# Penalties on another engine, low parts straight from the transposes, weight halves in pieces: one change to a fused FFT, gated-MLP and expert kernel

## The chip, the core and the metric

The kernel runs on one core of a Trainium2 chip. A core has five engines that run their own instruction streams and wait for each other by semaphores: PE (matmul; its weight loads are listed apart as PEld), DVE (vector), ACT (scalar, activation), POOL (GpSimd) and SP, which here only issues DMAs. The metric is the device time of one execution in microseconds; each kernel is run several times and the median counts. Lower is better.

## The reference

Three layers in a row, all in fp32. `B, S, D = 8, 3072, 256`, so 24,576 tokens of width 256.

```python
X = np.fft.fft(np.fft.fft(x, axis=1), axis=2).real          # (8, 3072, 256)
x = X.reshape(24576, 256)
g = x @ w_gate; y = (g * sigmoid(g) * (x @ w_val)) @ w_out   # hidden width 1536
logits = y @ gate2                                           # 8 experts
# experts fill up greedily: all (token, expert) pairs in falling order of logit,
# a token goes to the first expert that has room, each expert takes 24576/8 = 3072
for e in range(8):
    out[mask_e] = np.maximum(y[mask_e] @ w1[e], 0) @ w2[e]   # 256 -> 1024 -> 256
```

## The kernel before, in words

**Numbers as two parts.** Matmul operands are split into a rounded high part and a remainder, the low part (`hi = cast(x)`, `lo = x - hi`), and each product is the sum of three matmuls: high by high, high by low, low by high. So nearly every operand needs a cast (on ACT) and a subtraction (on POOL or DVE) before PE can read it.

**Phase 1** (48 tiles of 512 rows; 0 to about 1957 us) does the transforms, the gated MLP and the logits. A tile has 12 steps, one for each 128 hidden units. In a step PE computes the products `Q` and `Pp` and, three steps late, the output product of an earlier step into four PSUM tiles `Y`; DVE combines (`T`, `G`, `hh`), ACT does the Silu and the cast `hi`, POOL the subtraction `lo` (L691). After the twelfth step `finish(t, u)` runs for u = 0 to 3: ACT copies `Y` to `ys`; POOL copies the 8 logits into `Lall` (L425) and writes the token's number into column 256 of the row (L427); SP stores 128 rows to the DRAM table `yscr` (L430). POOL also does the folds of the next batch's input (`fa`, `fb`, `z`) and the low part `xl` of the next tile.

**Phase 2.** A search on DVE with small matmuls finds the threshold of the first expert to close, and the list of its 3072 tokens. From then on the eight experts run one after the other on PE, and the search for the next experts runs beside them. An expert has six groups of 512 tokens. For a group, POOL gathers 4 times 128 rows of `yscr` by index (L1075); `transpose` (L1081) turns them on PE into PSUM, ACT copies them to SBUF (`yt`) and casts (`yh`), POOL subtracts (`yl`, L1099); eight `up` products (L1111) with Relu on ACT (`hh`, L1117) and a low part on DVE (`hl`, L1128) follow, then four `down` products (L1137), whose results ACT copies and POOL scatters to the output (L1146). The weights of the next expert come by two gathers of 1 MB (`load_w`, L1059) and are split in eight pieces of 512 columns (`split_w`: cast on ACT, L1068; subtraction on POOL, L1069).

**The order of the work** is written out in program order, each engine in order. The search and the listing are generators; `go(time)`, called twice in an `up` and four times in a `down`, adds to a credit (at most 1.3) and runs a step of each generator while the credit lasts; a step yields its cost. An expert can't begin until its listing is done: at the end of the sixth group a loop calls `go(1.0)` until it is (the forced rest, `while ph + 1 not in ready`), ahead of that group's `down`s. When an expert is chosen, `close` (L1006) adds the penalty of the experts that are closed to all 24,576 x 8 logits, one POOL instruction (L1009), for the next search to read. The listing has 12 items: PE looks a row up (L1036), DVE turns it into two indices (`j`, `le`, `idx`, L1039 to L1047).

Of the kernel before, what the change touches and what calls it, by code (L numbers as in the profile page):

```python
# [9 lines left out]
F32 = mybir.dt.float32  # L10
F32R = mybir.dt.float32r
BF16 = mybir.dt.bfloat16
I32 = mybir.dt.int32
# [74 lines left out]
def phase1(ctx, tc, io, yscr, Lall, ident, idt, NT, choice=None):  # L88
# [321 lines left out]
    def out_proj(g):  # L410
# [4 lines left out]
        for u in range(4):  # L415
            for i, (a, d) in enumerate(((0, 0), (0, 1), (1, 0))):
                nc.tensor.matmul(Yp[t][u], h[a][:, u * P : (u + 1) * P], Wo[c // 2][:, c % 2, d, :], start=(c == 0 and i == 0), stop=(c == NF - 1 and i == 2))  # L417

    def finish(t, u):
        hf, q = (t // 3) % 2, t % 3  # L420
        pp = Yp[t][u]
        ys = work.tile([P, EXT], F32, tag="ys", bufs=4, name="ys")
        nc.scalar.copy(ys, pp)
        c = 4 * t + u
        nc.gpsimd.tensor_copy(Lall[:, c, :], ys[:, D:EXT])  # L425

        nc.gpsimd.tensor_copy(ys[:, D : D + 1].bitcast(I32), idt[:, c : c + 1])  # L427

        n = P - 1 if hf == 0 and q == 0 and u == 2 else P
        nc.sync.dma_start(yscr[c * P : c * P + n, :], ys[0:n, :])  # L430


    def mini_tile():

        xs = {}
        r0 = work.tile([1, B], F32, tag="tz", bufs=1, name="t15r")
        nc.sync.dma_start(r0, t15scr.rearrange("b o -> o b"))
        for n in ("R", "T"):
            for a in range(2):
                xs[n, a] = work.tile([P, P], F32R, tag=f"m{n}{a}", bufs=1, name=f"m{n}{a}")  # L440
                nc.gpsimd.memset(xs[n, a].bitcast(F32), 0.0)
        hs = [[work.tile([P, 4, P], F32R, tag=f"z{2 * j + a}", bufs=2, name=f"hT{a}") for a in range(2)] for j in range(3)]
        for t in hs:
            for a in range(2):
                nc.gpsimd.memset(t[a].bitcast(F32), 0.0)
        yield
        yield
        for n, src, k in (("R", mini["R"], P), ("T", r0, 1)):
            nc.vector.tensor_copy(xs[n, 0][0:k, 0:B], src)
            nc.vector.tensor_sub(xs[n, 1][0:k, 0:B], src, xs[n, 0][0:k, 0:B].bitcast(F32))  # L450
        yield
        for j in range(3):
            sl = work.tile([P, 4, D], F32, tag="xs", bufs=2, name="xs").rearrange("p a b -> p (a b)")
            for gv in range(2):
                pp = bank("F", 1)
                n = 0
                for cs, k in ((0, "R"), (1, "T")):
                    for a, d in order:
                        nc.tensor.matmul(pp, xs[k, d], Wb[j][:, cs, gv, a, :], start=(n == 0), stop=(n == 5))
                        n += 1  # L460
                yield
                if gv == 0:
# [12 lines left out]
        for _ in range(4):
            yield
        pp = bank("F", 1)
        for c in range(NF):
            for i, (a, d) in enumerate(((0, 0), (0, 1), (1, 0))):
                nc.tensor.matmul(pp[:, 0:EXT], hs[c // 4][a][:, c % 4, :], Wo[c // 2][:, c % 2, d, :], start=(c == 0 and i == 0), stop=(c == NF - 1 and i == 2))  # L480
            if c % 4 == 3 and c < NF - 1:
                yield
                yield
        yield
        ys = work.tile([B, EXT], F32, tag="ys", bufs=4, name="ysm")
        nc.vector.tensor_copy(ys, pp[0:B, 0:EXT])
        lm = work.tile([B, E], F32, tag="lm", bufs=1, name="lm")
        nc.vector.tensor_copy(lm, ys[:, D:EXT])
        nc.vector.tensor_copy(ys[:, D : D + 1].bitcast(I32), idt[0:B, NCOL : NCOL + 1])
        nc.sync.dma_start(yscr[3 * P - 1 : N : S, :], ys)  # L490
        nc.sync.dma_start(Lall[P - 1 : P, 2 : 4 * NT : 24, :], lm)
# [308 lines left out]
def phase2(ctx, tc, io, yscr, Lall, ident, first, out):  # L800
# [47 lines left out]
    def search(ph, res):  # L848
# [117 lines left out]
        if ph < E - 1:  # L966
            shut = rp.tile([P, E], F32, tag="shut", name="shut")
            nc.vector.tensor_scalar(shut, code8, best, -3.3e38, ALU.is_equal, ALU.mult)
            nc.vector.tensor_add(pen, pen, shut)
            if ph > 0:  # L970
                close(res)
        yield 1.2

        ise = rp.tile([P, NCOL], F32, tag="ise", name="ise")
# [31 lines left out]
    def close(res):  # L1006

        ml = rp.tile([P, NCOL, E], F32, tag="ml", name="ml")
        nc.gpsimd.tensor_add(ml, Lall, across(pen, NCOL))  # L1009
        res["next"] = ml  # L1010

    def listing(ph, res, first=None):
# [17 lines left out]
            yield 0.3  # L1030
        res["idx"] = []
        for i in range(NS // 2):
            pl = bank("A", 3) if first else bank("L", 1)
            v = pl.rearrange("p (a c) -> p a c", a=2)
            for a in range(2):
                nc.tensor.matmul(v[:, a, 0:XW], on[:, 2 * i + a, :], x, start=True, stop=True)  # L1036
            yield 0
            j = rp.tile([P, 2], F32, tag="j", bufs=2, name="j")
            nc.vector.tensor_sub(j, siota[:, 2 * i : 2 * i + 2], v[:, :, NCOL])  # L1039
            cc = rp.tile([P, 2], F32, tag="cc", bufs=2, name="cc")  # L1040
            for a in range(2):
                le = rp.tile([P, NCOL], F32, tag="le", bufs=2, name="le")
                nc.vector.tensor_scalar(le, v[:, a, 0:NCOL], j[:, a : a + 1], None, ALU.is_le, ALU.add, accum_out=cc[:, a : a + 1])
            if i % 2 == 0:
                res["idx"].append(rp.tile([P, 4], I32, tag=f"idx{i // 2}", bufs=2, name=f"idx{i // 2}"))
            k = 2 * (i % 2)
            nc.vector.scalar_tensor_tensor(res["idx"][-1][:, k : k + 2], cc, float(P), v[:, :, NCOL + 1], ALU.mult, ALU.add)  # L1047
            if first and i % 2:
                first(i // 2)
            yield 1.5  # L1050


    scat = []
    spacer = const.tile([P, 1], F32, name="spacer")

# [7 lines left out]
    def split_w(res, n):  # L1063

        j = len(res[f"w{n}"])
        f = res[f"w{n}f"][:, j * 512 : j * 512 + 512]
        h = wp.tile([P, 2, 512], F32R, tag=f"w{n}", bufs=5, name=f"w{n}")
        nc.scalar.copy(h[:, 0, :], f)  # L1068
        nc.gpsimd.tensor_sub(h[:, 1, :], f, h[:, 0, :].bitcast(F32))  # L1069
        res[f"w{n}"].append(h)  # L1070

    def gather(res, i):
# [5 lines left out]
            )  # L1078
        res["yg", i] = yg

    def transpose(res, i, k, first=False):  # L1081
        if k == 0:
            res["y", i] = tuple(work.tile([P, 2, 512], F32R, tag=t, bufs=2, name=t) for t in ("yh", "yl"))
        hi, lo = res["y", i]
        yg = res["yg", i]
        pt = bank("A", 3)
        for s in range(4):
            nc.tensor.transpose(pt[:, s * P : (s + 1) * P], yg[:, s, k * P : (k + 1) * P], ident)  # L1088
        if k == 1:
            res["id", i] = work.tile([P, 4], I32, tag="id", bufs=3, name="id")  # L1090
            nc.scalar.copy(res["id", i], yg[:, :, D].bitcast(I32))
        if first:
            nc.scalar.copy(hi[:, k, :], pt)
            nc.vector.tensor_sub(lo[:, k, :], pt, hi[:, k, :].bitcast(F32))
            return
        yt = work.tile([P, 512], F32, tag="yt", bufs=2, name="yt")
        nc.scalar.copy(yt, pt)
        nc.scalar.copy(hi[:, k, :], yt)
        nc.gpsimd.tensor_sub(lo[:, k, :], yt, hi[:, k, :].bitcast(F32))  # L1099

    order = ((0, 0), (1, 0), (0, 1))

# [77 lines left out]
    def begin(i):  # L1180
        if i == 0:
            gather(exp[0], 0)
            close(exp[0])

    for _ in listing(0, exp[0], begin):
        pass
    for _ in range(4):
        split_w(exp[0], 2)
    for k in range(2):
        transpose(exp[0], 0, k, True)  # L1190
    sides = [lists(), searches()]

    credit = 0.0

    def go(time):
# [7 lines left out]
    for ph in range(E):  # L1203
# [3 lines left out]
        for i in range(6):  # L1207
            if i < 5:
                gather(cur, i + 1)
            for f in range(8):  # L1210
# [8 lines left out]
                    since = 8 * i + f  # L1219

                if loaded:
                    for n, lag, free in ((1, 4, 1 if i < 5 else min(4, 1 + (f + 1) // 2)), (2, 8, 1)):
                        if 8 * i + f > since + lag and len(nxt[f"w{n}"]) < free:
                            split_w(nxt, n)
                if i == 5 and ph + 1 in ready and ("yg", 0) not in nxt:
                    gather(nxt, 0)
            if i == 5 and nxt is not None:
# [73 lines left out]
```

## Time and profile before

| | us |
|---|---|
| median of 3 runs | 3296.31 (3295.22 to 3297.11) |
| the profiled execution | 3293.48 |
| its span, first to last instruction | 3291.7 |
| phase 1, to the last output product | about 1956 |
| first search and listing, PE mostly idle | about 1957 to 2037 |
| eight experts | about 2037 to 3280 |

Busy times overlap between the engines, and a busy PE need not be at its peak. An idle time in square brackets in a timeline row is how long the engine stood still before the instruction, and the arrow what released it. The granted clock of PE is 1.00 at 2.4 GHz and 0.50 at 1.2 GHz.

### The profile page before, as it was taken

Reading aid. Unit: us, or ns where it says so; the run is one execution under the profiler, and the core shown is the slowest. Engines: PE = TensorE matmul, PEld = TensorE weight load, DVE = VectorE, ACT = ScalarE, POOL = GpSimd, SP = SyncE. Lnnn points to the kernel's source line nnn. Section 1 sums busy time; section 2 is a strip of 40 time slices with the busy share of each in tenths; the row PEclk is TensorE's granted clock in tenths of the full one; section 3 lists DMA queues with packets and bytes.
Section 4 is the critical chain, followed back from the end, with each engine's and each line's share of the span. In section 5 each row is a group of like instructions: output and inputs, shape, how many; then the busy total and the mean of one; then the engine's idle time right before and its main releaser. Section 6 shows DMA issues by size and latency. Waiting matters only on the chain.

```text
span 3291.7 us, 64128 instructions
## 1 busy us (share of the span) xinstructions
PE 3112.7 (95%) x23835; PEld 2936.8 (89%) x23835; DVE 2575.4 (78%) x5524; ACT 1565.5 (48%) x3080; POOL 1843.8 (56%) x2096
## 2 busy tenths in 40 slices
PE   5899999999999999999999985999999999999998
PEld 3799999999999999999999974888888888888998
DVE  7899999999999999999998898776676767664222
ACT  2556555555555555555565541333333333334343
POOL 4575675674764855856754443454555555555453
PEclk7999999999999999999999996999999999999999
DMA  5110100100100101101000001111111111122111
GB/s 204 30 37 18 44 31 23 51 24 24 49 20 30 47 21 37 37 18 45 31 24 11 25 26 41 62 42 65 40 66 41 67 41 66 40 71 68 49 45 38
DMA packets 73496, 144.00 MB, mean 44 GB/s; under 512 B 15650, under 2 KB 49490, under 8 KB 71136
## 3 DMA queue, kind: packets, MB, share of 16 engines
q1 hardware_dynamic: 52436, 71.97, 6.8%
q0 software_dynamic: 20736, 67.92, 6.2%
q8 instruction: 189, 3.10, 0.4%
q14 instruction: 123, 1.01, 0.1%
q10 hardware_dynamic: 12, 0.01, 0.0%
HBM read 88.67 MB, written 51.18 MB: 42 GB/s over the span
## 4 chain that ended last, share of the span: by engine, by line
PE 81%; issue 6%; POOL 5%; DVE 5%; ACT 1%; DMA 1%; SPq 0%; POOLq 0%; ACTq 0%; DVEq 0%
PE Y L417 22%; PE B L1137 16%; PE A L1111 14%; PE Q L386 11%; PE Pp L386 10%; PE F L326 2%; PE F L329 2%; POOL lo L691 2%; PE C L879 1%; PE A L1088 1%; POOL ys L427 1%; DVE T L397 1%; POOL xl L372 1%; DVE ge L871 1%; ACT qs L684 0%
## 5 line engine op out<-in xcount | busy, mean ns | idle before, releaser
L691 POOL TENSOR_TENSOR lo<-hh,hi 128x512 fp32r<-128x512 f32 x576 | 757.7, 1316 | 694.8 <-ACT hi L690 685.2
L417 PE MATMUL Y<-Wo,hi 128*128 128x264 f32 x4608 | 867.7, 284 | 0.0
L417 PEld LDWEIGHTS Y<-Wo,hi 128*128 128x128 f32 x4608 | 711.1, 188 | 0.2 <-ACT hi L690 0.2
L417 PE MATMUL Y<-Wo,lo 128*128 128x264 f32 x2304 | 659.6, 286 | 28.9 <-POOL lo L691 28.9
L397 DVE SCALAR_TENSOR_TENSOR T<-tb,w,Q 128x256 f32<-128x256 f32 x1152 | 501.2, 476 | 115.0 <-ACT qs L684 111.1
L684 ACT COPY qs<-Q 128x512 f32<-128x512 f32 x576 | 340.0, 590 | 519.6 <-PE Q L386 514.4
L1137 PE MATMUL B<-w,hh 128*128 128x256 f32 x3072 | 585.2, 290 | 0.0
L405 DVE TENSOR_TENSOR hh<-sl,G 128x512 f32<-128x512 f32 x576 | 501.3, 870 | 1.3 <-ACT sl L698 1.3
L1111 PE MATMUL A<-yh,w 128*128 128x512 f32 x1536 | 493.6, 403 | 3.1 <-DVE hl L1128 3.1
L1128 DVE SCALAR_TENSOR_TENSOR hl<-A,hh 128x512 fp32r<-128x512 f32 x384 | 262.8, 688 | 281.6 <-ACT hh L1117 253.5
L1137 PEld LDWEIGHTS B<-w,hh 128*128 128x128 f32 x3072 | 479.5, 192 | 3.3
L417 PEld LDWEIGHTS Y<-Wo,lo 128*128 128x128 f32 x2304 | 434.1, 188 | 36.7 <-POOL lo L691 34.2
L386 PE MATMUL Q<-xh,W 128*128 128x256 f32 x2304 | 446.2, 286 | 16.3 <-DVE T L397 8.1
L1146 POOL DMA_INDIRECT out_dram<-ot,id x192 | 198.8, 1036 | 457.2 <-ACT ot L1144 354.3
L1137 PE MATMUL B<-w,hl 128*128 128x256 f32 x1536 | 435.2, 283 | 7.5 <-DVE hl L1128 7.5
L386 PE MATMUL Pp<-xh,W 128*128 128x256 f32 x2304 | 431.0, 280 | 0.0
L690 ACT CAST hi<-hh 128x512 fp32r<-128x512 f32 x576 | 360.5, 626 | 77.6 <-DVE hh L405 72.1
L398 DVE TENSOR_TENSOR G<-Pp,qs 128x512 f32<-128x512 f32 x576 | 393.6, 683 | 0.0
L399 DVE TENSOR_TENSOR G<-T,Pp 128x512 f32<-128x512 f32 x576 | 390.6, 678 | 0.0
L1117 ACT ACTIVATE hh<-A 128x512 fp32r<-128x512 f32 x384 | 229.2, 598 | 329.5 <-PE A L1111 263.2
L386 PEld LDWEIGHTS Q<-xh,W 128*128 128x128 f32 x2304 | 354.4, 189 | 26.0 <-ACT hi L690 17.5
L698 ACT ACTIVATE sl<-G 128x512 f32<-128x512 f32 x576 | 365.4, 634 | 0.0
(256 smaller groups left out, 5305.2 us busy)
## 6 DMA issues: line engine op xcount, KB each, us to landing
yscr<-ys SPq DMA_DIRECT2D x184, 132.0 KB
xs<-in_x_dram SPq DMA_DIRECT2D x43, 512.0 KB
tb<-tscr SPq DMA_DIRECT2D x48, 128.0 KB
raw<-in_wg_dram SPq DMA_DIRECT2D x6, 512.0 KB
raw<-in_wv_dram SPq DMA_DIRECT2D x6, 512.0 KB
rawWo<-in_wo_dram SPq DMA_DIRECT2D x12, 256.0 KB
yg<-yscr,idx POOLq DMA_INDIRECT x192
out_dram<-ot,id POOLq DMA_INDIRECT x192
```

Source lines behind the costliest of these rows:

```text
L386: nc.tensor.matmul(pp[:, gv * 256 : gv * 256 + 256], W[:, cs, gv, a, cc : cc + P], RI[t][cs][d], start=(i == 0), stop=(i == 2))
L397: nc.vector.scalar_tensor_tensor(T[:, gv, :], tb, w2[:, gv, c : c + 1], pq[:, gv * 256 : gv * 256 + 256], op0=ALU.mult, op1=ALU.add)
L398: nc.vector.tensor_sub(G[:, 0, :], pp, qs)
L399: nc.vector.tensor_add(rev(G[:, 1, :])[:, :, ::-1], T, rev(pp))
L405: nc.vector.tensor_mul(hh, s["sl"], s["G"][:, :, 256:512])
L417: nc.tensor.matmul(Yp[t][u], h[a][:, u * P : (u + 1) * P], Wo[c // 2][:, c % 2, d, :], start=(c == 0 and i == 0), stop=(c == NF - 1 and i ...
L684: nc.scalar.copy(s["qs"], s["pq"])
L690: nc.scalar.copy(hi, s["hh"])
L691: nc.gpsimd.tensor_sub(lo, s["hh"], hi.bitcast(F32))
L698: nc.scalar.activation(s["sl"], s["G"][:, :, 0:256], AF.Silu)
L1111: nc.tensor.matmul(pa, w[:, a, c : c + P], res["y", i][d][:, k, :], start=(n == 0), stop=(n == 5))
L1137: nc.tensor.matmul(pb[:, 0:D], h[a][:, s * P : (s + 1) * P], w[:, d, (f % 2) * D : (f % 2) * D + D], start=(n == 0), stop=(n == 23))
```

## The change

1. `close` runs on ACT: eight activations, one for each expert, in place of one POOL addition, with a yield of cost 0 after each (so one each `go`).
2. `transpose`: ACT casts `yh` straight from PSUM, DVE subtracts from PSUM; the copy `yt` and POOL's subtraction go. `spend(0.7)` takes 0.7 from the credit for each.
3. `split_w`: POOL's subtraction in two pieces of 256 columns; the next expert's first splits come at the earliest 8 and 10 (before: 4 and 8) `up`s after the load, and no more than one an `up`.
4. `listing`: one more step of cost 0 ahead of items 2 to 12.
5. `finish`: the four `Y` copies go into one `ys` of 4 x 264 columns (one buffer); one POOL copy of logits and one of numbers, after the fourth; one store (three for each sixth tile).

```diff
     def finish(t, u):
-        ys = work.tile([P, EXT], F32, tag="ys", bufs=4, name="ys")
-        nc.scalar.copy(ys, pp)
-        c = 4 * t + u
-        nc.gpsimd.tensor_copy(Lall[:, c, :], ys[:, D:EXT])
-        nc.gpsimd.tensor_copy(ys[:, D : D + 1].bitcast(I32), idt[:, c : c + 1])
-        nc.sync.dma_start(yscr[c * P : c * P + n, :], ys[0:n, :])
+        if u == 0:
+            Ys[t] = work.tile([P, 4, EXT], F32, tag="ys", bufs=1, name="ys")
+        ys = Ys[t]
+        nc.scalar.copy(ys[:, u, :], Yp[t][u])
+        if u < 3:
+            return
+        c = 4 * t
+        nc.gpsimd.tensor_copy(Lall[:, c : c + 4, :], ys[:, :, D:EXT])
+        nc.gpsimd.tensor_copy(ys[:, :, D : D + 1].bitcast(I32), idt[:, c : c + 4].unsqueeze(2))
+        if t % 6:
+            nc.sync.dma_start(rows(0, 4), ys)
...
             if ph > 0:
-                close(res)
+                yield from close(res)
...
         ml = rp.tile([P, NCOL, E], F32, tag="ml", name="ml")
-        nc.gpsimd.tensor_add(ml, Lall, across(pen, NCOL))
+        for e in range(E):
+            nc.scalar.activation(ml[:, :, e], Lall[:, :, e], AF.Identity, bias=pen[:, e : e + 1])
+            yield 0
...
         for i in range(NS // 2):
+            if i and not first:
+                yield from wait(1)
...
         nc.scalar.copy(h[:, 0, :], f)
-        nc.gpsimd.tensor_sub(h[:, 1, :], f, h[:, 0, :].bitcast(F32))
+        for a in (0, 256):
+            nc.gpsimd.tensor_sub(h[:, 1, a : a + 256], f[:, a : a + 256], h[:, 0, a : a + 256].bitcast(F32))
...
-        yt = work.tile([P, 512], F32, tag="yt", bufs=2, name="yt")
-        nc.scalar.copy(yt, pt)
-        nc.scalar.copy(hi[:, k, :], yt)
-        nc.gpsimd.tensor_sub(lo[:, k, :], yt, hi[:, k, :].bitcast(F32))
+        nc.scalar.copy(hi[:, k, :], pt)
+        nc.vector.tensor_sub(lo[:, k, :], pt, hi[:, k, :].bitcast(F32))
+        spend(0.7)
...
-                    for n, lag, free in ((1, 4, 1 if i < 5 else min(4, 1 + (f + 1) // 2)), (2, 8, 1)):
+                    for n, lag, free in ((1, 8, 1 if i < 5 else min(4, 1 + (f + 1) // 2)), (2, 10, 1)):
                         if 8 * i + f > since + lag and len(nxt[f"w{n}"]) < free:
                             split_w(nxt, n)
+                            break
```

POOL at the end of a phase 1 tile, before: the last of the four pairs of logits copy and number cast, then a fold (`fb`), the next tile's `xl` and the step's `lo`.

```order
L425 COPY Lall<-ys 128x8
L427 CAST ys<-idt 128x1
L128 TENSOR_TENSOR fb<-fa 128x256
L372 TENSOR_TENSOR xl<-ab,xh 128x256
L691 TENSOR_TENSOR lo<-hh,hi 128x512
```

The same place now:

```order
L429 COPY Lall<-ys 128x32
L431 CAST ys<-idt 128x4
L128 TENSOR_TENSOR fb<-fa 128x256
L372 TENSOR_TENSOR xl<-ab,xh 128x256
L700 TENSOR_TENSOR lo<-hh,hi 128x512
```

Two instructions stand where eight did; what follows is the same.

DVE at the end of the first expert, before: the end of the forced rest, from the third of four listing items (`j`, `le`, `idx`) that stand between the `hl` of the seventh and of the eighth `up`; `tmp`, `red` and `sp` belong to the search beside it.

```order
L1039 TENSOR_TENSOR j<-cst,L 128x2
L1043 TENSOR_SCALAR le,cc<-L,j 128x192 x2
L1047 SCALAR_TENSOR_TENSOR idx_30938<-cc,L 128x2
L883 TENSOR_TENSOR tmp<-C,small 128x112
L885 TENSOR_REDUCE red<-tmp 128x7
L887 TENSOR_TENSOR sp<-red,small 128x56
L1039 TENSOR_TENSOR j<-cst,L 128x2
L1043 TENSOR_SCALAR le,cc<-L,j 128x192 x2
L1047 SCALAR_TENSOR_TENSOR idx_30938<-cc,L 128x2
L1128 SCALAR_TENSOR_TENSOR hl_30898<-A,hh_30897 128x512
```

The same place now, from the seventh of eight items:

```order
L880 TENSOR_TENSOR ge<-m,bits 128x336
L943 TENSOR_SCALAR base<-ktab,pre 128x7
L1052 TENSOR_TENSOR j<-cst,L 128x2
L1056 TENSOR_SCALAR le,cc<-L,j 128x192 x2
L1060 SCALAR_TENSOR_TENSOR idx_30424<-cc,L 128x2
L892 TENSOR_TENSOR tmp<-C,small 128x112
L894 TENSOR_REDUCE red<-tmp 128x7
L896 TENSOR_TENSOR sp<-red,small 128x56
L1052 TENSOR_TENSOR j<-cst,L 128x2
L1056 TENSOR_SCALAR le,cc<-L,j 128x192 x2
L1060 SCALAR_TENSOR_TENSOR idx_30424<-cc,L 128x2
L1143 SCALAR_TENSOR_TENSOR hl_30286<-A,hh_30285 128x512
```

Eight items (idx) in place of four now stand between the two `hl`, and with them almost two rounds of the search in place of one. The loop that forces them runs 25 times after the first expert (before: 8), and 2, 4, 4, 4, 4, 2 and 0 times after the next (before: 0).

POOL at the end of a later expert, the fourth, before: the gather of the next expert's first group, then three halves of `w1`.

```order
L1075 DMA yg<-yscr,idx_36334 128x264 x4
L1069 TENSOR_TENSOR w_37075<-w1f,w_37075 128x512
L1069 TENSOR_TENSOR w_37113<-w1f,w_37113 128x512
L1069 TENSOR_TENSOR w_37157<-w1f,w_37157 128x512
L1145 MEMSET spacer 128x1
```

Now:

```order
L1089 TENSOR_TENSOR w_36393<-w1f,w_36393 128x256 x2
L1089 TENSOR_TENSOR w_36427<-w1f,w_36427 128x256 x2
L1089 TENSOR_TENSOR w_36459<-w1f,w_36459 128x256 x2
L1095 DMA yg<-yscr,idx_35857 128x264 x4
L1160 MEMSET spacer 128x1
```

The gather now stands behind the three splits, because the listing is done only at the end of the last group.

## Rows read from the trace of the kernel before

**Rows 1.** Windows (us; busy by engine and instructions; clock; DMA share; GB/s).

```profile
500.00:1000.00 500.00, 491.02 (x4094) 487.45 (x4094) 463.11 (x853) 291.30 (x575) 314.57 (x355) 1.00 0.10 32
...
2060.00:2900.00 840.00, 805.97 (x5667) 711.73 (x5666) 591.77 (x1664) 291.02 (x566) 428.33 (x489) 0.98 0.16 54
...
2900.00:3280.00 380.00, 379.66 (x2520) 345.70 (x2520) 126.86 (x313) 149.67 (x292) 191.50 (x240) 1.00 0.16 53
```

**Rows 2.** PE's waits: for what, us in total, times, longest.

```profile
PE Y L417 <- POOL lo L691: 28.9, 25, 1.6
PE Q L386 <- DVE T L397: 8.1, 20, 1.5
```

**Rows 3.** Timeline (start, us, engine, line) of a tile's end in phase 1.

```profile
649.04 1.21 ACT L423 COPY ys<-Y 128x264 f32<-128x264 f32 x4
...
649.92 0.20 POOL L425 COPY Lall<-ys 128x8 f32<-128x8 f32 x1
...
653.31 1.73 POOL L691 TENSOR_TENSOR lo<-hh,hi 128x512 fp32r<-128x512 f32 x1
...
655.10 0.39 PE L417 MATMUL Y<-Wo,lo 128*128 128x264 f32 x1 [1.02 <-POOL lo L691]
```

**Rows 4.** Timeline, `ml` on POOL and `ise` on DVE; PE's first, last gap.

```profile
2014.97 0.31 DVE L975 TENSOR_SCALAR ise<-code,best 128x192 f32<-128x192 f32 x1
...
2891.03 3.55 POOL L1009 TENSOR_TENSOR ml<-Lall,pen 128x1536 f32<-128x1536 f32 x1 [4.15 <-DVE pen L969]
...
2891.46 3.24 DVE L975 TENSOR_SCALAR ise<-code,best 128x192 f32<-128x192 f32 x1
...
2134.11 0.39 PE L1137 MATMUL B<-w,hl 128*128 128x256 f32 x1 [3.15 <-DVE hl L1128]
...
2896.35 0.38 PE L1137 MATMUL B<-w,hl 128*128 128x256 f32 x1 [2.13 <-DVE hl L1128]
```

**Rows 5.** ACT's wait for `w1f` (total, times, longest); the two PE gaps behind it.

```profile
ACT w L1068 <- DMA w1f<-in_w_dram,wi: 14.6, 3, 7.0
...
2305.13 0.50 PE L1036 MATMUL L<-xrow,on 128*128 128x194 bf16 x2 [3.04 <-DVE idx L1047]
...
2761.22 0.34 PE L1036 MATMUL L<-xrow,on 128*128 128x194 bf16 x2 [2.74 <-DVE idx L1047]
```

**Rows 6.** Timeline, weight halves on POOL and `ge` on DVE; PE's first, last gap.

```profile
2830.98 4.03 DVE L871 TENSOR_TENSOR ge<-m,bits 128x560 bf16<-128x560 f32 x2
...
2831.36 2.50 POOL L1069 TENSOR_TENSOR w<-w1f,w 128x512 fp32r<-128x512 f32 x2
...
2212.72 0.51 PE L879 MATMUL C<-ge,oh 128*128 128x112 bf16 x5 [2.12 <-DVE ge L871]
...
2834.53 0.42 PE L879 MATMUL C<-ge,oh 128*128 128x112 bf16 x5 [2.11 <-DVE ge L871]
```

**Rows 7.** Windows of PE at the first gap of rows 4 (busy, matmuls, clock).

```profile
2136.00:2137.00 1.00, 1.00 (x6) 0.50 1.03 434
...
2139.00:2140.00 1.00, 1.00 (x11) 1.00 0.97 410
...
2130.00:2140.00 10.00, 6.85 (x47) 0.83 0.56 207
```

**Rows 8.** Timeline of PE, first and last gap in the first expert's forced rest.

```profile
2183.50 0.34 PE L1036 MATMUL L<-xrow,on 128*128 128x194 bf16 x2 [1.35 <-DVE idx L1047]
...
2186.67 0.50 PE L1036 MATMUL L<-xrow,on 128*128 128x194 bf16 x2 [1.10 <-DVE idx L1047]
```

**Rows 9.** A gather's last issue on POOL, and windows of DMA behind it.

```profile
2044.86 0.95 POOL L1075 DMA_INDIRECT yg<-yscr,idx  x1 [0.30 <-issue]
...
2047.50:2048.00 0.50, 0.00 (x0) 1.00 0.17 33
```

**Rows 10.** Lines by form: busy us, mean ns of one.

```profile
L1094 DVE TENSOR_TENSOR yl<-A,yh 128x512 fp32r<-128x512 f32 x2 | 1.4, 692 | 0.1
...
L1024 ACT CAST xrow<-R 128x193 bf16<-128x193 f32 x8 | 2.6, 319 | 1.3 <-DVE begin L1022 1.3
```

More of the change, by code (lines that the diff above doesn't have):

```diff
@@ L417, in out_proj @@
                 nc.tensor.matmul(Yp[t][u], h[a][:, u * P : (u + 1) * P], Wo[c // 2][:, c % 2, d, :], start=(c == 0 and i == 0), stop=(c == NF - 1 and i == 2))
+    Ys = {}
     def finish(t, u):
-        hf, q = (t // 3) % 2, t % 3
-        pp = Yp[t][u]
-        ys = work.tile([P, EXT], F32, tag="ys", bufs=4, name="ys")
-        nc.scalar.copy(ys, pp)
-        c = 4 * t + u
-        nc.gpsimd.tensor_copy(Lall[:, c, :], ys[:, D:EXT])
-        nc.gpsimd.tensor_copy(ys[:, D : D + 1].bitcast(I32), idt[:, c : c + 1])
-        n = P - 1 if hf == 0 and q == 0 and u == 2 else P
-        nc.sync.dma_start(yscr[c * P : c * P + n, :], ys[0:n, :])
+        if u == 0:
[7 more added lines that the diff above has]
+        nc.gpsimd.tensor_copy(ys[:, :, D : D + 1].bitcast(I32), idt[:, c : c + 4].unsqueeze(2))
+        rows = lambda a, n: yscr[(c + a) * P : (c + a + n) * P, :].rearrange("(u p) d -> p u d", p=P)
+        if t % 6:
+            nc.sync.dma_start(rows(0, 4), ys)
+        else:
+            nc.sync.dma_start(rows(0, 2), ys[:, 0:2, :])
+            nc.sync.dma_start(yscr[(c + 2) * P : (c + 3) * P - 1, :], ys[0 : P - 1, 2, :])
+            nc.sync.dma_start(rows(3, 1), ys[:, 3:4, :])
     def mini_tile():
@@ L484, in mini_tile @@
         yield
-        ys = work.tile([B, EXT], F32, tag="ys", bufs=4, name="ysm")
+        ys = work.tile([B, EXT], F32, tag="ys", bufs=1, name="ysm")
         nc.vector.tensor_copy(ys, pp[0:B, 0:EXT])
@@ L1050, in listing, with spend @@
             yield 1.5
+    credit = 0.0
+    def spend(time):
+        nonlocal credit
+        credit -= time
     scat = []
@@ L1079, in gather, with transpose @@
         res["yg", i] = yg
-    def transpose(res, i, k, first=False):
+    def transpose(res, i, k):
         if k == 0:
@@ L1091, in transpose @@
             nc.scalar.copy(res["id", i], yg[:, :, D].bitcast(I32))
[L1092 to L1095, printed above, removed]
-        yt = work.tile([P, 512], F32, tag="yt", bufs=2, name="yt")
-        nc.scalar.copy(yt, pt)
-        nc.scalar.copy(hi[:, k, :], yt)
-        nc.gpsimd.tensor_sub(lo[:, k, :], yt, hi[:, k, :].bitcast(F32))
+        nc.scalar.copy(hi[:, k, :], pt)
+        nc.vector.tensor_sub(lo[:, k, :], pt, hi[:, k, :].bitcast(F32))
+        spend(0.7)
     order = ((0, 0), (1, 0), (0, 1))
@@ L1182, in begin @@
             gather(exp[0], 0)
-            close(exp[0])
+            for _ in close(exp[0]):
+                pass
     for _ in listing(0, exp[0], begin):
@@ L1189, in phase2 @@
     for k in range(2):
-        transpose(exp[0], 0, k, True)
+        transpose(exp[0], 0, k)
     sides = [lists(), searches()]
```

## The prediction

> **What bounds the kernel now.** I read the busy time by stage first, then PE's waits and gaps, then the timeline around each kind of gap. In phase 1 PE is busy 491 of 500 us and DVE 463, so DVE is close behind; in the experts while searches run PE is busy 806 of 840 us at a mean clock of 0.98, and once they are over 379.7 of 380 [rows 1]. PE is the bound everywhere but in the first search (which the change leaves as it is), and a change off PE can win only the gaps: 9 us in 500 of phase 1, 34 us from 2060 to 2900, and what a lowered clock costs behind them.
>
> Phase 1's gaps have one large row, PE on POOL's `lo`: 28.9 us in 25 waits; DVE's `T` adds 8.1 [rows 2]. At a tile's end ACT's four copies end at 649.04 + 1.21 = 650.25, POOL begins its eight small instructions at 649.92, comes to `lo` only at 653.31, and PE stands 1.02 us for it [rows 3].
>
> The experts' gaps come in three kinds. While POOL adds the penalties (3.55 us), DVE's `ise`, 0.31 us in the first search where POOL rests, takes 3.24; the low part queued behind it is late, and PE waits. Six gaps are of this sort (in one it is POOL's `yl`): 3.15, 2.19, 2.20, 3.11, 2.27 and 2.13, together 15.05 us; the first and the last are shown [rows 4]. ACT, in order, waits at a weight cast for `w1f`, 14.6 us in three times, and two PE gaps follow, 3.04 and 2.74 [rows 5]. Two weight halves back to back on POOL (2.50 us) hold DVE's `ge` (two in 4.03 us), and the count that reads it stops PE: 2.12, 2.10, 1.27, 2.11, 2.11, together 9.71 us [rows 6]. Behind a gap the clock can fall: after the 3.15 us at 2131 to 2134 PE does 6 matmuls in a microsecond at 0.50 instead of 11 at 1.00, and the 10 us around it have a mean of 0.83, so about 3.4 us at 1.2 GHz [rows 7].
>
> **The change part by part**, against the profiled execution (3293.48 us, 1.8 outside its span, 2.8 below the median).
>
> *Tile ends.* Six fewer POOL instructions of 0.20 us are 1.2 us; the first must now wait for ACT's fourth copy, 0.3 us later than today [rows 3]. `lo` comes 0.9 us earlier, at most 25 x 0.9 = 22 us. What hides nothing here is next in line: DVE, 93% busy, whose `T` stops PE already, and PE that comes earlier finds it later. I take 5 us back: -17. Bounds: 0 (DVE takes it all) and -25. That one `ys` buffer serves all tiles costs nothing: its store has a tile's 38 us. The single store takes three issues from SP, which nobody waits for.
>
> *Penalties on ACT.* POOL's additions go, and `yl` on POOL too, so all six gaps of the kind: -15.05. In return ACT gets 56 activations of 192 columns; nearest is its copy of 193 columns, 0.319 us [rows 10], so 18 us over seven searches, on an engine busy 291 of 840 us [rows 1] which at the same time loses 94 copies. Behind the first of each eight, which waits for `pen` on DVE, stands the Relu of the eighth `up`; the `down` needs that one only at its 22nd matmul, so I give it nothing (bounds 0 and 1 us each).
>
> *Splits.* With 8 `up`s between load and first split ACT's wait goes: -5.8. The `w1` halves no longer stand behind the next expert's gather, and come one an `up`; so three of the five `ge` gaps (5.5) go. The two at `w2` halves remain behind a gather. There the row speaks against the pieces: `ge`, begun 0.4 us before the first half, was not done until both halves were [rows 6], so a run of pieces may hold it as long as two whole ones did. Bounds for these two gaps are 0 and their 4.2 us; I take half, -2.1, which makes -7.6 for `ge` in all (bounds -5.5 and -9.7). The Trainium skill ("SBUF — State Buffer", section "SBUF: two separate sides") says that DVE and GpSimd share a port pair which is locked for one whole instruction by whichever starts first; by that rule DVE would get in behind a single piece, both gaps would go and the sum would be 2.1 us lower. Two whole halves in a row, as in [rows 6], don't agree with it.
>
> *Clock.* Nine dips like that of [rows 7] stand behind these gaps and the forced rest. One costs 3.4 x (11 - 6)/11 = 1.55 us. The two at the forced rest stay; of the other seven I count six gone: -9.3 (0 to -10.9).
>
> *DVE's new load.* 94 subtractions of 0.692 us [rows 10], 65 us, bring DVE from 592 of 840 us [rows 1] to 657 at most, fewer waits apart; `spend` takes the side work back as much. A group's second `yl` is made while PE does the last `down`, 24 matmuls at 11 to a us, 2.2 us; cast and subtraction take 1.3. I take +3 in all; bounds 0 and 47 groups x 0.3 = 14.
>
> *The forced rest.* Here the change costs. Each activation and each extra step takes a `go`, and spent credit takes more: the listing of the second expert is later, eight items in place of four stand in the rest, and PE can't pass them. Today's three gaps there are 1.35, 1.04 and 1.10 [rows 8], 3.49 us. Seven gaps at that mean make 8.1, +4.7; the search's rows between the items (almost two rounds for one) lengthen each, at most double: +12.8. I take +7.5. In the five later rests one item or none is left, on DVE's time: 0.
>
> *The gather behind the splits.* At the end of experts 2 to 6 the next group's gather is now issued after the last group's splits. A gather takes four issues of 0.95 with 0.30 between, its last issue begins at 2044.86 and its data moves until the window that ends at 2048.00 [rows 9]: 4 x 1.25 + 2.2 = 7.2 us from the first issue, 7.4 from the last `up` by my count of POOL's queue. PE wants it two `down`s (48 matmuls, 4.4 to 5.7 us) and the rest's PE work later. So about 0.8 us each, 5 x 0.8 = +4; bounds 0 and 5 x 2.5 = +12.
>
> Sum: -17 - 15.05 - 5.8 - 7.6 - 9.3 + 3 + 7.5 + 4 = -40.3, 3253.2 us by the profiled execution; the median stands 2.8 higher: **3256 us**.
>
> **The rivals.**
>
> *DVE takes phase 1's gain.* DVE is 93% busy there and its `T` stops PE 20 times [rows 2]. For it: these waits come soon after the `lo` gaps. Against it: between the two DVE is seen idle for ACT. If 2 of the 17 us remain: 3271.
>
> *The ends of the experts cost more.* If each gather is 2.5 us late and the clock falls behind it (5 x 4.05, for the 4 us counted) and the first rest goes to its bound: +16 and +5: 3277. For it: the loop now runs at six of seven ends. Against it: POOL has less queued, and the gap that lasted 1.27 us [rows 6] had no dip.
>
> *The low parts on DVE come late (slower).* Each of 47 groups waits at its start for `yl`, since DVE in order must first do side work, and two steps of about 1 us may stand in front. It decides as soon as a group's wait is 0.9 us on the mean (40.3 / 47); at 1.3 us the kernel takes 3256 + 61 = 3317. For it: DVE is the busiest engine beside PE in that stage [rows 1]. Against it: the 0.9 us of room between 2.2 and 1.3.
>
> *The change does less than it says*: pieces and lags do nothing, the `ge` and `w1f` gaps and their dips stay (7.6 + 5.8, and three dips, 4.7): 3274.
>
> *More than I grant*: all lower bounds (tile ends -25, `ge` -9.7, forced rest +4.7, gather and DVE 0): 20 us less, 3236.
>
> **How the numbers follow.** My forecast has 0.53; DVE in phase 1 0.15, the ends 0.10, late low parts 0.05, less than it says 0.05, more 0.12. The likeliest case alone spans 3247 to 3266 by its own terms. For eight in ten I take in the two dearer faster cases and most of the better one: 3240 to 3279. No change means within 0.2%, 6.6 us, which is about what a measurement of this kernel can tell. Slower needs the late low parts nearly in full or several costs at once: 0.04; no change 0.05; faster 0.91.
>
> **What would show each step.** Right: PE's waits for `lo` in phase 1 fall from 28.9 to under 10 us, with `T`'s 8.1 not above 15; no gap of PE behind `ise`, `sel` or `fin`, which take 0.3 to 0.5 us; no row of ACT waiting for `w1f`; `yl` on DVE at 0.69 us with PE not waiting for it; one run of gaps of 9 to 14 us between `idx` at the end of the first expert; gaps of about 1 us at the first transposes of later experts; fewer dips from 2060 to 2900. Wrong: `T` or `hl` at the head of PE's waits, or gaps at the start of most groups, which would be DVE as the bound.

## The result, and the profile after

| | before | after |
|---|---|---|
| median of 4 runs each, one chip | 3295.76 us (3295.13 to 3297.11) | 3237.39 us (3236.59 to 3237.68) |
| ratio, 95% interval | | 0.9822 [0.9805, 0.9839] |
| span of the profiled run | 3291.7 us | 3235.9 us |
| start to first transpose of the experts (phase 1, first search) | 2035.2 us | 2004.0 us, -31.2 |
| from there to the end (experts) | 1256.5 us | 1231.9 us, -24.6 |

Forecast was 3256 us, 3240 to 3279: right in direction, 19 us short, and the time lies 2.6 us below the range. The experts came close to the forecast (-24.6 for -23.25); phase 1 gave 31 us where I had granted 17.

The windows of the changed kernel, in the columns of [rows 1] (phase 1, then the experts with searches):

```profile
500.00:1000.00 500.00, 497.68 (x4170) 495.84 (x4169) 464.38 (x870) 296.30 (x584) 306.44 (x279) 1.00 0.10 31
2030.00:2870.00 840.00, 822.49 (x5845) 725.43 (x5844) 587.25 (x1732) 285.49 (x570) 349.01 (x476) 0.99 0.17 57
```

PE's idle time fell from 9 to 2.3 us in the first and from 34 to 17.5 in the second; POOL lost 79 us in the second, and DVE is no busier than before (587 us for 592). PE's waits of the changed kernel answer to [rows 2]:

```profile
PE Q L386 <- DVE T L397: 6.8, 19, 0.4
PE L L1049 <- DVE idx L1060: 6.6, 7, 1.9
PE Y L417 <- POOL lo L700: 5.5, 11, 1.3
```

The wait for `lo` is nearly gone and `T` did not grow. A tile's end on the timeline of the changed kernel, the tile of [rows 3]:

```profile
639.12 1.21 ACT L425 COPY ys<-Y 128x264 f32<-128x264 f32 x4
...
640.39 0.55 POOL L429 COPY Lall<-ys 128x32 f32<-128x32 f32 x1 [0.32 <-ACT ys L425]
...
641.00 0.19 POOL L431 CAST ys<-idt 128x4 int32<-128x4 int16 x1
...
642.54 1.29 POOL L700 TENSOR_TENSOR lo<-hh,hi 128x512 fp32r<-128x512 f32 x1
...
643.14 1.25 DVE L405 TENSOR_TENSOR hh<-sl,G 128x512 f32<-128x512 f32 x1
643.31 0.59 ACT L693 COPY qs<-Q 128x512 f32<-128x512 f32 x1 [1.14 <-PE Q L386]
...
644.00 0.28 PE L417 MATMUL Y<-Wo,lo 128*128 128x264 f32 x1
...
647.51 0.59 ACT L693 COPY qs<-Q 128x512 f32<-128x512 f32 x1 [0.49 <-PE Q L386]
```

and three rows of the timeline before which were not shown yet:

```profile
653.06 0.85 DVE L405 TENSOR_TENSOR hh<-sl,G 128x512 f32<-128x512 f32 x1
...
653.23 0.59 ACT L684 COPY qs<-Q 128x512 f32<-128x512 f32 x1 [1.14 <-PE Q L386]
...
658.72 0.59 ACT L684 COPY qs<-Q 128x512 f32<-128x512 f32 x1 [0.50 <-PE Q L386]
```

There is one `qs` a step, so the distance of two starts is the length of a step whatever PE's modelled ends say. This step took 5.49 us before and takes 4.20 now: 1.29, though the idle time shown was 1.02 [rows 3]. Over all 575 steps, three tile ends a batch (those during which POOL folds the next batch), 21 in all, became 1.29 shorter (1.01 to 1.56), 27 us; 25 others 0.15 each, 3.8 us, though no idle time had been shown there. Measured from `qs`, `lo` ran from 0.08 to 1.81 before [rows 3], now from -0.77 to 0.52: it starts 0.85 us earlier and is 0.44 us shorter. Before, it began 0.25 us behind DVE's `hh`; now it begins ahead of `hh`, which takes longer instead (1.25 us for 0.85).

In the experts, the timeline of the changed kernel where [rows 4] stood, in the sixth search:

```profile
2862.82 2.47 ACT L1019 ACTIVATE ml<-Lall,pen 128x192 f32<-128x192 f32 x4
2863.55 0.35 DVE L984 TENSOR_SCALAR ise<-code,best 128x192 f32<-128x192 f32 x1
```

No PE gap is left behind `ise`, and none behind `w1f`. The end of the first expert (PE's first and longest gap at its listing, against [rows 8]); the first gap at the weight pieces (against [rows 6]); the late gather; and a row that is new, DVE 2.82 us idle with no releaser in this profile ("remote"). There are three such rows, called the late starts below:

```profile
2149.72 0.34 PE L1049 MATMUL L<-xrow,on 128*128 128x194 bf16 x2 [1.19 <-DVE idx L1060]
...
2157.34 0.50 PE L1049 MATMUL L<-xrow,on 128*128 128x194 bf16 x2 [1.91 <-DVE idx L1060]
...
2474.99 0.21 DVE L913 TENSOR_REDUCE mx<-R 128x7 f32<-128x56 f32 x1 [2.82 <-remote]
...
2491.24 5.14 POOL L1089 TENSOR_TENSOR w<-w2f,w 128x256 fp32r<-128x256 f32 x6
...
2492.60 1.82 DVE L880 TENSOR_TENSOR ge<-m,bits 128x560 bf16<-128x560 f32 x2
...
2494.95 1.81 DVE L880 TENSOR_TENSOR ge<-m,bits 128x336 bf16<-128x336 f32 x1
...
2496.81 0.31 PE L888 MATMUL C<-ge,oh 128*128 128x112 bf16 x3 [1.22 <-DVE ge L880]
...
2940.36 0.33 PE L1108 MATMUL A<-ident,yg 128*128 128x128 f32 x1 [0.52 <-DMA yg<-yscr,idx]
```

Eight gaps from 2148 to 2161 sum to 8.86 us, four like that of 2496.81 to 4.85. The clock by windows (last columns clock, DMA share, GB/s):

```profile
2104.00:2204.00 100.00, 90.63 (x639) 79.00 (x638) 73.85 (x221) 31.38 (x65) 43.51 (x61) 0.93 0.17 58
2150.00:2166.00 16.00, 9.21 (x62) 7.35 (x60) 13.89 (x69) 0.22 (x1) 2.20 (x4) 0.57 0.11 30
2204.00:2304.00 100.00, 99.96 (x699) 89.31 (x698) 68.38 (x200) 35.51 (x71) 39.94 (x54) 1.00 0.19 65
```

After the experts' start, the one lowered stretch begins in the forced rest; every later window of 100 us has 1.00, up to 3204, and the clock falls again only at 3228.6, behind PE's last matmul.

### The profile page after: what moved, and what is told of

The parts are those of the page before. It is cut to its first block, busy times and chain, and to the rows that moved or that the text cites. A ratio compares the mean times of both kernels' runs of the same rounds, so it can differ in the third digit from the quotient of the medians.

```text
span 3235.9 us, 63224 instructions
## 1 busy us (share of the span) xinstructions
PE 3097.4 (96%) x23835; PEld 2925.1 (90%) x23835; DVE 2564.9 (79%) x5618; ACT 1532.9 (47%) x3042; POOL 1667.1 (52%) x1771
## 4 chain that ended last, share of the span: by engine, by line
PE 85%; DVE 6%; issue 5%; POOL 2%; ACT 1%; DMA 0%; another core or an unknown queue 0%; SPq 0%; POOLq 0%; ACTq 0%; DVEq 0%
PE Y L417 23%; PE B L1152 15%; PE A L1126 15%; PE Q L386 12%; PE Pp L386 11%; PE F L326 2%; PE F L329 2%; PE A L1108 1%; PE C L888 1%; DVE T L397 1%; DVE ge L880 1%; POOL lo L700 1%; DVE G L399 1%; DVE le L1056 0%; DVE hl L1143 0%
## 5 line engine op out<-in xcount | busy, mean ns | idle before, releaser
L700 POOL TENSOR_TENSOR lo<-hh,hi 128x512 fp32r<-128x512 f32 x576 | 745.8, 1295 | 701.7 <-ACT hi L699 688.7
L1152 PE MATMUL B<-w,hh 128*128 128x256 f32 x3072 | 575.7, 287 | 0.0
L1161 POOL DMA_INDIRECT out_dram<-ot,id x192 | 192.3, 1001 | 590.6 <-ACT ot L1159 456.5
L405 DVE TENSOR_TENSOR hh<-sl,G 128x512 f32<-128x512 f32 x576 | 475.9, 826 | 1.3 <-ACT sl L707 1.3
```

What stands on the lines that cost most here:

```text
L405: nc.vector.tensor_mul(hh, s["sl"], s["G"][:, :, 256:512])
L700: nc.gpsimd.tensor_sub(lo, s["hh"], hi.bitcast(F32))
L1152: nc.tensor.matmul(pb[:, 0:D], h[a][:, s * P : (s + 1) * P], w[:, d, (f % 2) * D : (f % 2) * D + D], start=(n == 0), stop=(n == 23))
```

## The experiments

**Which half gave what.** Four kernels: the tile ends alone, all but them, and the tile ends with only the copies or only the store merged. Beside the runs of this section the kernel before took 3294.88 to 3296.61 us (medians), so less than about 2 us between two runs says little.

```
e1: before + new finish()          e2: after, with finish() of before
e3: e1, but  for v in range(4): dma_start(yscr[... c + v ...], ys[0:n, v, :])
e4: e1, but for each u:
+   tensor_copy(Lall[:, c + u, :], ys[:, u, D:EXT])
+   tensor_copy(ys[:, u, D:D+1], idt[:, c+u : c+u+1])
```

> The kernel before with only the new tile ends of phase 1 (one ys tile, two POOL copies in place of eight, one store). Phase 1 ended 31.1 us earlier after the whole change, where I had granted 17. Theory A (the tile ends give all of it: each of 21 tile ends where POOL folds gave 1.28 us from one start of qs to the next, where PE's shown idle was 1.02): 3296 - 31 = 3265 us, no T wait of PE above 9 us in phase 1. Rival B (the tile ends give the 17 that I had granted, the other 14 come from somewhere else in the change): 3279 us.

> The changed kernel with the tile ends of before (eight POOL copies, four stores). Theory A (phase 1 is changed by the tile ends alone and the experts by the rest, so the two add): 3237.4 + 31 = 3268.5 us, experts 24.6 us shorter than before as in the whole change, PE's wait for lo in phase 1 back at 29 us. Rival B (14 us of phase 1's gain come from elsewhere): 3255 us.

> As the tile ends alone, but with four stores: only POOL's eight copies are merged into two. Theory A (what counts is when POOL comes to lo): as the tile ends alone, 3265 us. Rival C (the store matters: four DMA issues and four semaphores, or what they do to POOL's copies): 3280 to 3296 us.

> As the tile ends alone, but with POOL's eight copies kept: only the store is one. Theory A: as before, 3296 us, within 2 us, with PE's wait for lo at 29 us. Rival C (the store matters): 3265 to 3280 us.

Against 3294.88 before: e1 3263.06 us (0.9901 [0.9884, 0.9917]), e2 3264.82 (0.9905 [0.9889, 0.9922]), e3 3264.24 (0.9906 [0.9889, 0.9922]), e4 3295.39 (1.0001 [0.9991, 1.0010]). PE's waits, of e1 and then of e4:

```profile
PE Q L386 <- DVE T L397: 8.3, 20, 1.5
PE Y L417 <- POOL lo L700: 5.5, 11, 1.3
```

```profile
PE Y L417 <- POOL lo L699: 28.8, 25, 1.6
```

Theory A stands, B and C fall: POOL's copies carry all of phase 1's gain, the store none. Only the sum is off: e1 and e2 give 31.8 and 30.1 us, together 3.5 more than the whole change. e2's experts take 1227.8 us, the whole change's 1231.9; the late starts, which e2 does not have, make that difference (see e16).

**What a stall of PE costs.** Two or four more copies of 0.19 us at each tile end.

```
+ for _ in range(2):   # and 4
+     nc.gpsimd.tensor_copy(ys[:, :, D : D + 1], idt[:, c : c + 4])
```

> The changed kernel with two more small POOL copies (0.19 us each) at each tile end of phase 1, so that lo starts 0.38 us later. In the changed kernel lo ended at 643.83 and PE came to it at 644.00. Theory A (a stall of PE costs more than the idle time shown: the lateness, and 0.11 us because the matmul behind a stall takes 0.39 in place of 0.28): 21 tile ends x (0.38 - 0.17 + 0.11) = +6.7 us, 3244 us, while the shown wait for lo rises by only about 1 us. Rival G (the idle time shown is the price): +1 us, 3238.5 us.

> The same with four more copies: lo would start 0.76 us later, at 643.30, just after DVE's hh at 643.14. Theory A (whichever of hh and lo starts first makes the other one wait: lo then ends 0.68 us behind it, as in the kernel before, where it took 1.73 in place of 1.29): the whole 1.28 us of each tile end comes back at once, 21 x 1.28 = +27 us, 3264 us, wait for lo 25 us or more. Rival D (each copy costs its own 0.19 us and lo keeps its 1.29 us): 21 x (0.76 - 0.17 + 0.11) = +15 us, 3252 us, wait for lo about 14 us.

3247.10 us (0.9852 [0.9837, 0.9867]) and 3271.35 (0.9926 [0.9910, 0.9941]). The same tile end on the timeline, e5_plus2 and then e5_plus4:

```profile
647.75 1.29 POOL L702 TENSOR_TENSOR lo<-hh,hi 128x512 fp32r<-128x512 f32 x1
...
647.84 1.75 DVE L405 TENSOR_TENSOR hh<-sl,G 128x512 f32<-128x512 f32 x1
...
649.10 0.39 PE L417 MATMUL Y<-Wo,lo 128*128 128x264 f32 x1 [0.24 <-POOL lo L702]
```

```profile
655.84 1.00 DVE L405 TENSOR_TENSOR hh<-sl,G 128x512 f32<-128x512 f32 x1
...
656.25 1.73 POOL L702 TENSOR_TENSOR lo<-hh,hi 128x512 fp32r<-128x512 f32 x1
...
658.03 0.39 PE L417 MATMUL Y<-Wo,lo 128*128 128x264 f32 x1 [1.17 <-POOL lo L702]
```

| this tile end | idle shown | PE's `Y` on `lo` late by | step longer than after |
|---|---|---|---|
| +2 copies | 0.24 | 0.39 | 0.50 |
| before (eight copies) | 1.02 | 1.18 | 1.29 |
| +4 copies | 1.17 | 1.32 | 1.44 |

"Late" is against the 0.25 us that separate it from the first `hi` matmul where nothing waits. In all three the step grows by the lateness and 0.11 or 0.12 (the matmul behind a stall takes 0.39 for 0.28), and by the idle time shown and 0.26 to 0.27. G and D fall: time to the first transpose rose by 13.5 and 38.6 us, where shown waits rose by 9.8 and 26.4. My numbers for A were low (6.7 and 27): four copies take 0.95 us, not 0.76, and the tile ends without folds lose 0.30 each at +4. In the tile end shown, `lo` is still ahead of `hh` with two copies (1.29) and behind it with four (1.73, as before). With two it had already fallen behind at 7 of the 21 (1.72 to 1.74): their steps grew by 0.94, the other 14 by 0.50. The whole kernels grew by less, 9.7 and 34.0, since their experts have no late starts.

**Penalties back on POOL.** `for e: scalar.activation(ml[:, :, e], ...); yield 0` becomes `gpsimd.tensor_add(ml, Lall, across(pen, NCOL)); yield 0`.

> The changed kernel with the penalties back on POOL as one addition of 3.55 us, all else as changed. Theory A (POOL's one long addition holds DVE's ise as in the kernel before, and PE waits for the low part behind it): five or six PE gaps of 2 to 3 us behind it come back, +12 to +15 us, with lower clock behind some of them +3 to +6, less 3 us of a shorter forced rest (20 steps in place of 25): 3250 to 3256 us. Rival H (those gaps came from the low parts of the gathered rows on POOL, which stay on DVE here): 3235 to 3240 us, no gap behind ise.

3246.90 us (0.9851 [0.9836, 0.9866]): 9.5 more than the whole change, 3 us under A's range and 7 above H's. From here on no kernel has the late starts, so e16 below (3233.25), the whole change without them, is the closer one to compare with: e6 is 13.7 above it, as A's terms say (+12 to +18). A's mechanism is there in all six, [rows 4] again on the timeline of e6: four `ise` take 3.2 to 3.6 us, and where `ise` begins ahead of the addition, `sel` behind it takes 3.6. The PE gaps behind the six sum to 11.6 us, where 15.05 stood before:

```profile
2101.13 3.60 DVE L988 SCALAR_TENSOR_TENSOR sel<-m,last,ise 128x192 f32<-128x192 f32 x1
...
2242.20 3.53 POOL L1018 TENSOR_TENSOR ml<-Lall,pen 128x1536 f32<-128x1536 f32 x1 [5.28 <-DVE pen L978]
2242.64 3.21 DVE L984 TENSOR_SCALAR ise<-code,best 128x192 f32<-128x192 f32 x1
...
2247.50 0.38 PE L1151 MATMUL B<-w,hl 128*128 128x256 f32 x1 [2.94 <-DVE hl L1142]
```

**Weight halves whole.** `for a in (0, 256)` out, one `tensor_sub` of 512 columns.

> The changed kernel with each low weight half on POOL in one instruction of 1.25 us in place of two pieces. In the changed kernel a run of six pieces at the start of an expert still leaves a PE gap of 1.21 us behind DVE's ge, four times. Theory A (back-to-back POOL instructions hold DVE's ge whether they are pieces or not; what removed the other ge gaps is that w1 halves now come one an up): no more than 2 us from the changed kernel's 3237 us. Rival I (the pieces let ge in, whole halves don't): the four gaps grow to 2.1 and gaps return at the w1 halves, +5 us or more, 3242 us and above.

3245.84 us (0.9848 [0.9832, 0.9864]), 8.5 above the whole change and 12.6 above e16: A falls. Timeline of e8 at the start of the third expert:

```profile
2496.91 2.35 DVE L880 TENSOR_TENSOR ge<-m,bits 128x560 bf16<-128x560 f32 x2
2497.22 1.55 POOL L1088 TENSOR_TENSOR w<-w2f,w 128x512 fp32r<-128x512 f32 x1 [0.87 <-ACT w L1087]
...
2497.69 0.42 PE L888 MATMUL C<-ge,oh 128*128 128x112 bf16 x5 [1.69 <-DVE ge L880]
...
2499.31 0.36 PE L888 MATMUL C<-ge,oh 128*128 128x112 bf16 x4 [0.44 <-DVE ge L880]
```

Per expert 2.13 us of gap for 1.22, a 2.05 us gap at 2185.84 as well, and four of 0.74 to 1.36 behind `hl`. So pieces are worth something, but two `ge` beside them still take 1.82 us and one of 336 columns 1.81, where 0.49 is what it takes at 2499.78 in e8. Pieces in a row can hold `ge` nearly as long as whole halves did: in e11 below, four in a row leave a gap of 1.73 or 1.74 at each of four experts (before: 2.1):

```profile
2484.61 2.81 POOL L1089 TENSOR_TENSOR w<-w2f,w 128x256 fp32r<-128x256 f32 x4
...
2485.50 2.53 DVE L880 TENSOR_TENSOR ge<-m,bits 128x560 bf16<-128x560 f32 x1
...
2488.09 0.42 PE L888 MATMUL C<-ge,oh 128*128 128x112 bf16 x5 [1.74 <-DVE ge L880]
```

**Lags of before.** `(1, 8, ...), (2, 10, 1)` back to 4 and 8, `break` out.

> The changed kernel with the waits between weight load and first split as before (4 and 8 ups, both splits in one up allowed), pieces kept. Theory A (ACT waits for w1f because the split comes too early): ACT's wait for w1f returns, two or three times, PE gaps of 2 to 3 us behind it, +5 to +6 us, and w1 pieces behind the next expert's gather bring some ge gaps of 1.2 us back: 3242 to 3246 us. Rival J (the load now comes early enough by itself): no wait for w1f, 3236 to 3239 us.

3238.45 us (0.9824 [0.9808, 0.9840]). Neither theory holds as told. ACT waits for `w1f` once, where A said two or three times and J none, and the PE gaps behind it are small:

```profile
2122.59 0.62 ACT L1087 CAST w<-w1f 128x512 fp32r<-128x512 f32 x1 [3.45 <-DMA w1f<-in_w_dram,wi]
...
2123.76 0.50 PE L1152 MATMUL B<-w,hh 128*128 128x256 f32 x2 [0.48 <-ACT hh L1132]
```

With a second one of 0.22 that is 0.7 us, so most of the 5.8 us did not need the lags. Which other part brought the loads forward was not separated. Against e16, which like e9 has no late starts, it is 5.2 us slower: so the lags and the `break` are worth something in another way; four new gaps of 0.64 behind `hl` are about half of it.

**Low parts back on POOL; charge out.** e10: `scalar.copy(yt, pt)`, cast and `gpsimd.tensor_sub` as before. e13: only `spend(0.7)` out.

> The changed kernel with the gathered rows as before (ACT copies PSUM to yt, casts yt, POOL subtracts; nothing charged). Theory A (DVE's new 65 us lie beside PE's work, and POOL's subtraction was at fault in one gap only): POOL and ACT get back 94 instructions each, DVE loses them, the forced rest is shorter (20 steps for 25, none at the later experts): 3233 to 3241 us. Rival K (POOL's longer queue makes low parts and gathers late): PE waits for yl or yg, 3245 us and above.

> The changed kernel with its low parts on DVE but no charge to the side work for them (spend taken out). The steps of side work are then given out as in the run with the rows through yt (20 steps in the first forced rest, none later). Theory A (that run's 7 us came from the pace of the side work, not from the engine of the subtraction): 3229 to 3232 us. Rival L (they came from DVE's 65 us): 3236 us or more, with PE waiting for hl, ge or yl.

3230.22 us (0.9798 [0.9783, 0.9814]) and 3232.41 (0.9805 [0.9792, 0.9818]). For e13 A's range holds within half a microsecond and L falls. 2.2 us lie between the two places of the subtraction, with the two kernels' single runs overlapping, so a small loss from the low parts on DVE is likely and not shown by this pair alone. e10 came out better than either theory said. Both kernels lack the late starts, which is most of their 5 to 7 us. Against e16, which has the charge and lacks the late starts too, e13 is 0.8 us faster, so A's reason, the pace of the side work, gave next to nothing.

**The forced rest.** e7: `wait(1)` out of the listing, activations in two groups of four, charge 0.35. e11: `credit + 1.3 * time` in the first expert. e14, e15: e10 with 1.3 and with 1.7.

> The changed kernel with a shorter forced rest: the listing takes one step less per item, the eight activations are given out in two steps in place of eight, and a transposition is charged 0.35 in place of 0.7. At the end of the first expert 10 steps are then left in place of 25, at the later ones none in place of 2 to 4. Theory A (the rest costs what its steps wait for): the run of gaps there falls from 8.9 us to about 4, and one dip of the clock with it: 3230 to 3233 us. Rival F (less time set aside for DVE's new load makes its low parts late): PE waits for hl or yl, 3237 us or more.

> The changed kernel with the side work of the first expert given out 1.3 times as fast, later experts as changed: 10 steps stand in the forced rest at the end of the first expert in place of 25. Theory A (the rest costs what its steps wait for, and DVE has room in the first expert): the run of gaps there falls from 8.9 us to about 4, 3230 to 3234 us. Rival F (side work that comes faster makes DVE's low parts late): PE waits for hl or yl in the first expert, 3237 us or more.

> The changed kernel with the gathered rows through yt and POOL again, and the side work of the first expert given out 1.3 times as fast: 7 steps in the forced rest. Theory A (the rest costs what its steps wait for, 8.5 us of gaps in the run through yt with 20 steps): gaps of about 3 us there and a shorter dip, 3222 to 3225 us. Rival F (faster side work makes DVE's low parts late in the first expert): 3228 us or more.

> The same at 1.7 times: no step is left in the forced rest. Theory A: no gap there and no dip, 3219 to 3222 us. Rival F (faster side work makes DVE's low parts late in the first expert): PE waits for hl, 3225 us or more.

e7 3243.33 us (0.9840 [0.9826, 0.9853]): its rest fell to 5.3 us of gaps, but a new wait came that neither theory named, 5.0 us of gaps behind ACT's `ot` and `yh` in four places. Its timeline:

```profile
2102.01 4.53 ACT L1019 ACTIVATE ml<-Lall,pen 128x192 f32<-128x192 f32 x8 [2.52 <-DVE pen L978]
...
2106.85 0.51 PE L1151 MATMUL B<-w,hh 128*128 128x256 f32 x2 [1.79 <-ACT ot L1158]
```

Activations without a step between them keep ACT from `ot`, which frees PE's bank. That price I had put at 0 to 1 us; with one step an activation, as in the whole change, no such gap is seen. e7 changed three things at once, so the rest of its loss is not divided among them. e11 3228.94 us (0.9793 [0.9780, 0.9807]): three gaps in the rest, 2.9 us, in place of 8.86, and 4.3 us under e16. e14 3223.65 us (0.9780 [0.9767, 0.9794]), the fastest, 13.7 us under the whole change (9.6 under e16): one gap in the rest, its window 2104 to 2204 at clock 1.00. It differs from e11 in the low parts on POOL and their charge alone, and is 5.3 us faster. e15 3230.28 us (0.9801 [0.9787, 0.9814]): no gap in the rest, but rival F holds, and nothing is left of the gain over e10:

```profile
2120.85 1.28 DVE L1148 SCALAR_TENSOR_TENSOR hl<-A,hh 128x512 fp32r<-128x512 f32 x2
...
2121.59 0.72 PE L1131 MATMUL A<-yh,w 128*128 128x512 f32 x2 [2.90 <-DVE hl L1148]
```

**The late starts.** Two more copies where t % 6 > 2.

```
+ for _ in range(2 if t % 6 > 2 else 0):
+     nc.gpsimd.tensor_copy(ys[:, :, D : D + 1], idt[:, c : c + 4])
```

> The changed kernel with two more small POOL copies at the 24 tile ends of phase 1 without folds, where two more had cost nothing, so that POOL's list of instructions is longer and the time of phase 1 the same. Theory M (the three late starts hang on where POOL's list stands): experts 4 to 5 us shorter, 3233 us. Theory N (they hang on something else): 3237 us, as the changed kernel.

3233.25 us (0.9811 [0.9796, 0.9826]); first transpose at 2004.36 as after, experts 1227.0 us, and no such late `mx`. First its row at the place of the first late start: it begins 0.04 us behind the end of the matmul that it reads, where the whole change's began 2.19 us behind. Then the PE gap behind that late start in the whole change:

```profile
2471.49 0.22 DVE L915 TENSOR_REDUCE mx<-R 128x7 f32<-128x56 f32 x1 [0.67 <-PE R L902]
```

```profile
2476.63 0.42 PE L888 MATMUL C<-ge,oh 128*128 128x112 bf16 x5 [0.90 <-PE B L1152]
```

N falls: with 48 more POOL instructions and the same phase 1 the three late starts (`mx` at 2474.99, 2630.16, 2785.34, and `ot` with it), which cost 0.90, 0.87 and 1.02 us of shown PE gap, are gone. But M is not the whole of it: e9, e11 and e13 have phase 1's instructions as the whole change has them, differ from it in the experts alone, and have no late starts either. So changes in either place remove them. What they are stays open; no other run has the rows.

## Why the prediction was wrong

*Tile ends* is the step that failed: -17 taken, -31 measured, bound -25. Three errors, all in one direction. I took `lo` to end as much earlier as it starts (0.9 us; 0.85 measured) and did not see that its 1.73 us in [rows 3] held 0.44 of waiting for `hh`. "A change off PE can win only the gaps" took the shown idle time as a stall's whole price, which is 0.27 more, and the 0.15 at 25 tile ends that show no idle time at all was not in the count: 21 x 1.29 and 25 x 0.15 make the 31. And I gave 5 us back to DVE: `T` went from 8.1 to 6.8. So the rival in which DVE takes the gain is wrong, and "more than I grant" is right for phase 1 alone. That its 3236 is 1.4 us from the time measured is luck: its `ge` (-9.7) and its rest (+4.7) were not reached, and the late starts were in no term.

*Penalties on ACT* (-15.05): the gaps went. The activations take about 0.62 us each in a row of them, not 0.319 (row at 2862.82), 34 us in all instead of 18; no PE gap follows them.

*Splits*: `w1f` (-5.8) went. `ge` fell from 9.71 to 4.85 us, -4.9 for -7.6. The three gaps at `w1` halves went, as said, but the two at `w2` halves, of which I had given the pieces half, became four of 1.2 us, at four experts. The Trainium skill ("SBUF — State Buffer", section "SBUF: two separate sides") says that the port pair shared by DVE and GpSimd is locked for one whole instruction by whichever starts first. By that rule `ge` would get in behind a single piece. The trace agrees only in part: two `ge` were done between the six pieces, but the one begun at 2494.95 only 0.4 us behind the last piece. e8 shows that the pieces count.

*Clock* (-9.3): worked out from the clock of the twelve windows of 100 us from the first transpose on, 17 us under full speed in sum before, 10 now: 7. The shown gaps fell by 16.9 of 24.6, which leaves 7.7.

*DVE's load* (+3): one gap of 0.3 us behind `hl`. In time it was 2.2 between e10 and e13, and with the charge 5.3 between e11 and e14. *Gather* (+4): 0.5. *Forced rest* (+7.5): 8.86 - 3.49 = +5.4. The seven gaps between the eight items make 7.85 (8.1 at the mean of before), so the search's rows did not lengthen them on the mean; the eighth gap, 1.01, waits for the search's `ge`. e11 and e14 show that much of it can be had back.

What no row of the kernel before showed: the late starts, +2.8 in shown gaps and +4.7 in the experts (1231.9 against 1227.2, the mean of e2, e16 and the two e5). The experts' forecast came out close by luck: these, `ge` and the clock used up what the gather, DVE's load and the rest did not cost.

## What to carry to other kernels

In this kernel the idle time shown before a matmul was a lower bound of a stall: measure the step between two markers off PE (here the starts of `qs`) and compare steps with and without it. When an instruction reads longer than its like (1.73 for 1.29), look for what it waited for inside: moving its start may change who waits, so the gain comes as a step and not in proportion. Side work given out by credit is best tuned at the few places where the rest is forced, not everywhere: here 1.3 there gained (4.3 us, e11 against e16; 6.6, e14 against e10), 1.7 gained nothing (e15 against e10), and e7 with fewer steps lost.

## What was not expected of the hardware

- Behind a stall a 128x264 matmul reads 0.39 for 0.28 us. At 25 tile ends the step became 0.15 us shorter where the profile had shown no idle time of PE.
- POOL's `lo` and DVE's `hh`, each alone 1.29 and 0.68 us, run nearly one after the other. In e5_plus2 `lo` starts 0.09 us earlier and `hh` takes 1.75; in e5_plus4 `hh` starts 0.41 us earlier and `lo` takes 1.73.
- An ACT activation of 192 columns that reads and writes every eighth element takes 0.57 to 0.62 us in a row of them (4.53 for eight); a copy of 193 adjacent ones took 0.319 [rows 10]. That the stride is the reason was not tested.
- 48 small POOL instructions far earlier moved the experts by 5 us, with PE's and DVE's instructions the same.
